# Taking kv from the value weights as column-group pairs, and moving five small transfers up the sync queue

## The chip, the cores and the metric

The kernel runs on one core of one Trainium2 chip. The metric is device time in microseconds (us), the median of several executions. The start of each matmul is recorded to a few nanoseconds.

## The reference, cut to what matters

The kernel computes `g * A(x) + (1 - g) * B(x)` for 2048 tokens of width 640. Path B is a two-layer mixer and MLP. Path A is linear attention with 32 heads of 20:

```python
qkv = (x @ wqkv) ...                      # 32 heads, Dh = 20
pq, pk = phi(q), phi(k)
kv  = einsum("bhsd,bhse->bhde", pk, v)    # one 20 x 20 matrix per head
num = einsum("bhqd,bhde->bhqe", pq, kv)
den = einsum("bhqd,bhd->bhq", pq, z) + 1e-6
A   = (num / den).reshape(B, S, D) @ wo
```

As v = x wv, kv per head is wv^T (x^T pk). The kernel builds `GT` = x^T pk once (640 x 640). It then takes only blocks of 60 x 60 (three heads) of wv^T GT, masks them to single heads (`Lt`), and multiplies them by wo, giving one matrix M. With M, path A is one matrix product per tile of normalised queries.

## The kernel before

The kernel has its own scheduler: work items are put in program order by their dependencies, and each engine is given its list in that order. TensorE runs the projections, GT, kv and M, then the MLP; ten "a" matmuls per token tile of 128 (two groups of five, for 512 and for 128 columns) apply M. The parts the change touches follow.

ScalarE copies the value weights into a regrouped form, so that one full 128-column weight load holds two blocks at rows 0 and 64:

```python
def wv_blocks(k):                 # 5 copies for each of 5 k: 25 ScalarE instructions
    ...
    activation(wv2[:, k, e:e + 2 * ns - 1:2, 64 * h:64 * h + 64], src, ACTF.Copy)
```

Then kv comes in two items, with another matmul group between them:

```python
KV0 = (0, 60, 240, 300, 480, 540)
def kvt_group(h):
    ...
    for q_, g in enumerate(range(4) if h == 0 else range(4, 6)):
        for k in range(KD):                       # KD = 5
            l = wv2[:, k, g, :]                   # 128 weight columns
            # 120 moving columns (two blocks), or 160, or 60
```

Of each 128 x 120 product only the two diagonal 60 x 60 blocks are used.

The last rows of M (the tail of each head pair) are computed into a small tile `Mt` and brought to rows 60 to 67 of `M_sb` by five transfers of 10 KB on the sync queue (SP). The same queue issues the DMA transposes of the normalised x (`xnT<-xn`) and of the queries (`pqnT<-pq_tok`, one per token tile):

```python
def m_tail():
    for j in range(KD):
        sch.dma("sp", M_sb[60:68, j, :], Mt[8 * j:8 * j + 8, :], "mt", group_total=KD)
...
IT.add("MT", ("mt",), 0.0, m_tail, deps=[(("m", 1), 1.5), (("qt", 5), 0.0)])   # behind the 6th query transpose
```

The first "a" group reads all of `M_sb`, so it waits for these five.

## Time and profile before

| what | value | from |
|---|---|---|
| time | 262.55 us, median of 3 | times |
| TensorE busy | 257.3 us of 261.4 (98%) | page, part 1 |
| kv matmuls | 1.05 + 0.48 = 1.53 us | starts in the trace |
| wait for M's last rows | 0.94 us | starts in the trace |
| ScalarE copies of the weights | 6.5 us | groups by form |

The page of the kernel before, part 1 (busy us, share, number of instructions) and part 4 (the chain that ended last):

```profile
PE 257.3 (98%) x1665; PEld 133.9 (51%) x1665; DVE 151.7 (58%) x289; ACT 112.1 (43%) x241; POOL 93.0 (36%) x152
...
PE 96%; DMA 2%; SPq 0%; DVE 0%; ACT 0%; issue 0%
```

TensorE is the bound; only what shortens its list, or a wait in it, can shorten the run. Busy time of a pipelined matmul overlaps its neighbours' (379 ns are recorded for one of 512 columns), so a better reading is the step from one matmul's start to the next: 216 ns for 512 columns, 56 ns for 128. Where a step is longer, TensorE waited, or it entered or left another form of its array (309 to 312 ns, see the prediction).

The timeline of TensorE around kv (start, us, engine, line, operation, shapes, count):

```profile
76.64 1.03 PE L601 MATMUL ps<-xnT,w 128*128 128x512 bf16 x4
77.50 1.21 PE L974 MATMUL ps<-GT,wv 128*128 128x120 bf16 x20
78.55 1.24 PE L601 MATMUL ps<-xnT,w 128*128 128x512 bf16 x5
79.63 0.65 PE L974 MATMUL ps<-GT,wv 128*128 128x160 bf16 x10
80.11 1.24 PE L601 MATMUL ps<-xnT,w 128*128 128x512 bf16 x5
```

Read the starts: kv takes 77.50 to 78.55 and 79.63 to 80.11.

The sync queue (timeline of SP) and TensorE around the first "a" group, then the waits that name the transfers:

```profile
123.41 3.08 SPq L281 DMA_TRANSPOSE xnT<-xn  x2
126.53 9.00 SPq L281 DMA_TRANSPOSE pqnT<-pq_tok  x6
135.66 4.13 SPq L285 DMA_DIRECT2D M_sb<-Mt  x5
139.88 2.54 SPq L281 DMA_TRANSPOSE xnT<-xn  x2
```

```profile
136.63 3.62 PE L601 MATMUL ps<-xnT,w 128*128 128x512 bf16 x16
141.03 1.53 PE L601 MATMUL ps<-M_sb,pqnT 128*128 128x512 bf16 x10 [0.78 <-DMA M_sb<-Mt]
```

```profile
PEld ps L601 <- DMA M_sb<-Mt: 1.3, 1, 1.3
...
PE ps L601 <- DMA M_sb<-Mt: 0.8, 1, 0.8
```

Six query transposes stand ahead of the transfers in the queue, though the first "a" group needs only one of them. The last matmul before the wait starts at 139.87, the next at 141.03: 1156 ns where 216 would do, so 0.94 us is lost. (The 0.78 of the view is counted from the modelled end of a matmul.)

### The profile page before, as it was taken

How to read it: one execution, taken by the hardware profiler on the slowest of the kernel's cores; microseconds unless marked ns; L12 is line 12 of the kernel's file. 1: busy time of each engine (PE TensorE's matmuls, PEld its weight loads, DVE VectorE, ACT ScalarE, POOL GpSimd, SP SyncE). 2: the span in 40 equal slices, each digit the busy share in tenths (PEclk: the TensorE clock that was granted, in tenths of full speed). 3: DMA queues.
4: the chain of work that ended last, by engine and by line, in shares of the span. 5: the costliest groups of instructions: out<-in, count | busy, mean ns of one | idle time of the engine just before them, and what ended most of it. 6: DMA issues, size and time to landing. Idle time of an engine off the chain costs nothing.

```text
span 261.4 us, 4276 instructions
## 1 busy us (share of the span) xinstructions
PE 257.3 (98%) x1665; PEld 133.9 (51%) x1665; DVE 151.7 (58%) x289; ACT 112.1 (43%) x241; POOL 93.0 (36%) x152
## 2 busy tenths in 40 slices
PE   8999999999999999999998999999999999999996
PEld 4655555554455555554444545654455644455453
DVE  1497787899903799998996406993023320133232
ACT  1386767759355766685853240005500035200000
POOL 4003996869864019667901401130011110021001
DMA  6865869582656991362572670123000020000211
GB/s 196 256 103 143 165 173 171 168 142 42 107 107 125 354 332 31 74 104 51 110 95 58 125 78 0 25 65 113 0 3 0 0 103 0 0 3 1 100 53 50
DMA packets 51348, 24.99 MB, mean 96 GB/s; under 512 B 42708, under 2 KB 49917, under 8 KB 51328
## 3 DMA queue, kind: packets, MB, share of 16 engines
q1 hardware_dynamic: 49952, 21.31, 35.4%
q0 software_dynamic: 1136, 3.28, 5.6%
q8 instruction: 13, 0.21, 0.3%
q10 hardware_dynamic: 240, 0.13, 0.2%
q14 instruction: 7, 0.06, 0.1%
HBM read 12.05 MB, written 2.62 MB: 56 GB/s over the span
## 4 chain that ended last, share of the span: by engine, by line
PE 96%; DMA 2%; SPq 0%; DVE 0%; ACT 0%; issue 0%
PE ps L601 60%; PE ps L1176 22%; PE ps L783 8%; PE ps L875 2%; DMA wq<-in_A_wqkv_dram 1%; PE ps L1088 1%; PE ps L1158 1%; DMA M_sb<-Mt 1%; PE ps L974 1%; PE ps L876 1%; SPq L285 0%; DVE x_tok L640 0%; PE ps L1006 0%; PE ps L612 0%; ACT h2T L657 0%; PE ps L1155 0%
## 5 line engine op out<-in xcount | busy, mean ns | idle before, releaser
L601 PE MATMUL ps<-xnT,w 128*128 128x512 bf16 x360 | 81.6, 379 | 0.0
L657 ACT ACTIVATE h2T<-ps 128x512 bf16<-128x512 f32 x52 | 30.5, 598 | 68.5 <-PE ps L601 68.5
L1176 PE MATMUL ps<-w,h2T 128*128 128x512 bf16 (+1 forms) x416 | 58.8, 299 | 0.0
L601 PEld LDWEIGHTS ps<-xnT,w 128*128 128x128 bf16 x360 | 34.2, 98 | 38.2 <-issue 0.9
L640 DVE SCALAR_TENSOR_TENSOR x_tok<-ps,stg,abx 128x512 bf16<-128x512 f32 (+1 forms) x32 | 17.3, 550 | 61.1 <-PE ps L1176 61.1
L623 POOL TENSOR_SCALAR abx<-x_tok,stg 128x640 f32<-128x640 bf16 x16 | 14.8, 928 | 97.5 <-DVE x_tok L640 94.2
L1176 PEld LDWEIGHTS ps<-w,h2T 128*128 128x128 bf16 x416 | 32.1, 98 | 24.9 <-issue 1.1
L623 POOL TENSOR_SCALAR xn<-x_tok,st 128x640 bf16<-128x640 bf16 x32 | 34.5, 1086 | 17.9 <-DMA xnT<-xn 17.2
L657 ACT ACTIVATE Er<-ps 128x640 bf16<-128x640 f32 x32 | 22.5, 705 | 18.5 <-PE ps L876 8.6
L601 PE MATMUL ps<-M_sb,pqnT 128*128 128x512 bf16 (+1 forms) x160 | 24.4, 299 | 0.8 <-DMA M_sb<-Mt 0.8
L656 ACT ACTIVATE junk<-x_tok 128x640 bf16<-128x640 bf16 x32 | 23.6, 737 | 3.1 <-DVE x_tok L638 2.6
L657 ACT ACTIVATE hsT<-ps 128x512 bf16<-128x512 f32 (+1 forms) x32 | 18.9, 593 | 13.4 <-PE ps L601 13.0
L601 PE MATMUL ps<-w,hsT 128*128 128x512 bf16 (+1 forms) x160 | 23.7, 299 | 0.0
L601 PE MATMUL ps<-wkg,xT 128*128 128x512 bf16 (+1 forms) x150 | 22.6, 299 | 0.0
L640 DVE SCALAR_TENSOR_TENSOR abx<-ps,stg,abx 128x640 f32<-128x640 f32 x16 | 14.1, 884 | 14.4 <-PE ps L601 7.4
L601 PEld LDWEIGHTS ps<-w,hsT 128*128 128x128 bf16 x160 | 13.3, 98 | 12.2
L601 PEld LDWEIGHTS ps<-M_sb,pqnT 128*128 128x128 bf16 x160 | 13.1, 98 | 11.9 <-DMA M_sb<-Mt 1.3
L601 PE MATMUL ps<-wq,xT 128*128 128x512 bf16 (+1 forms) x120 | 18.3, 299 | 0.0
L783 PE MATMUL ps<-pk_tok,x_tok 128*128 128x512 bf16 x80 | 17.8, 379 | 0.0
L623 DVE TENSOR_SCALAR Er<-Er 128x640 bf16<-128x640 bf16 x32 | 11.6, 362 | 9.4 <-ACT Er L657 9.2
L601 PEld LDWEIGHTS ps<-wkg,xT 128*128 128x128 bf16 x150 | 12.2, 97 | 9.0
L638 DVE SCALAR_TENSOR_TENSOR x_tok<-ps,x_tok 128x640 bf16<-128x640 f32 x16 | 13.1, 820 | 6.0 <-PE ps L601 5.1
(76 smaller groups left out, 241.1 us busy)
## 6 DMA issues: line engine op xcount, KB each, us to landing
w<-in_B_w_dram SPq DMA_DIRECT2D x1, 2160.0 KB, 8.2
w<-in_B_w_dram SPq DMA_DIRECT2D x1, 2080.0 KB, 15.1
x_tok<-in_A_x_dram SPq DMA_DIRECT2D x3, 640.0 KB, 5.7
out_dram<-x_tok SPq DMA_DIRECT2D x3, 640.0 KB, 3.1
w<-in_B_w_dram POOLq DMA_DIRECT2D x8, 160.0 KB, 4.4
wq<-in_A_wqkv_dram SPq DMA_DIRECT2D x5, 160.0 KB, 3.9
wkg<-in_A_wqkv_dram SPq DMA_DIRECT2D x5, 160.0 KB, 3.9
wv<-in_A_wqkv_dram POOLq DMA_DIRECT2D x1, 800.0 KB, 6.1
```

What stands on the lines that cost most here:

```text
L601: ins = e.matmul(out_ap, l, r, start=(i == 0), stop=(i == n - 1))
L623: return engf(lambda e: e.tensor_scalar(out_ap, in_ap, s1, s2, op0, op1), rd, [out_ap], cost=cost)
L638: return dve(lambda e: e.scalar_tensor_tensor(out_ap, in0, scalar, in1, op0, op1, accum_out=accum), rd, [out_ap, accum], cost=cost + 70.0)
L640: return dve(lambda e: e.scalar_tensor_tensor(out_ap, in0, scalar, in1, op0, op1), rd, [out_ap], cost=cost)
L656: return act(lambda e: e.activation(out_ap, in_ap, func, bias=bias, scale=scale, accum_out=accum), rd, wr, cost=cost)
L657: return act(lambda e: e.activation(out_ap, in_ap, func, bias=bias, scale=scale), rd, wr, cost=cost)
L783: ins = e.matmul(o, l, r, start=(t0 + q_ == 0), stop=(t0 + q_ == NT - 1))
L875: e.matmul(ps[:, b, 0:512], l, w[:, k, 0:512], start=(k == 0), stop=(k == KD - 1))
L876: return e.matmul(ps[:, b + 1, 0:n2], l, w[:, k, 512:512 + n2], start=(k == 0), stop=(k == KD - 1))
L974: ins = e.matmul(o, l, r_, start=st_, stop=sp_, skip_group_check=True)
L1088: ins = e.matmul(o, l, r, start=st, stop=sp)
L1176: ins = e.matmul(o, l, r, start=False, stop=(i == KFF - 1), skip_group_check=(n0 > 0))
```

## The change

Two things at once. First, kv: no regrouped copy. Each 60-row block takes 64 columns of the value weights where they lie; two blocks go to output rows 0 to 63 and 64 to 127, that is to two column groups of the array, which are meant to run at the same time. Second, the five transfers go behind the third query transpose instead of the sixth.

```diff
-    wv2 = ra.alias("wv2", [128, KD, 6, 128], BF16, ...)
...
-    def wv_blocks(k): ...            # and its 5 work items
...
-    KV0 = (0, 60, 240, 300, 480, 540)
+    KV0 = ((0, 120), (60, 180), (240, 360), (300, 420), (480, 600), (540, None))
-    def kvt_group(h):
+    def kvt_group():
...
+        for g, cs in enumerate(KV0):
             for k in range(KD):
-                l = wv2[:, k, g, :]
...
+                for h, c0 in enumerate(cs):
+                    if c0 is not None:
+                        n = min(B3, D - c0)
+                        mms.append((ps[64 * h:64 * h + 64, b, B3 * g:B3 * g + n], wvf[:, D * k + c0:D * k + c0 + 64],
+                                    GT[:, k, c0:c0 + n], g == 0 and k == 0, k == KD - 1))
...                                   # taking kv out of PSUM: 5 VectorE instructions instead of 7
-    IT.add("MT", ("mt",), 0.0, m_tail, deps=[(("m", 1), 1.5), (("qt", 5), 0.0)])
+    IT.add("MT", ("mt",), 0.0, m_tail, deps=[(("m", 1), 1.5), (("qt", 2), 0.0)])
...
-        IT.add("QT", ("qt", t), ..., deps=[...])
+        IT.add("QT", ("qt", t), ..., deps=[...] + ([(("mt",), 0.0)] if t == 3 else []))
```

More of the change, by code (lines that the diff above doesn't have):

```diff
@@ L495, in _build @@
     GT = ra.alias("GT", [128, KD, D], BF16, ra.last_addr, KD * S * 2)
-    wv2 = ra.alias("wv2", [128, KD, 6, 128], BF16, ra.last_addr + KD * D * 2, KD * (S - D) * 2)
     wkg = ra.alloc("wkg", [128, KD, NK], BF16)
@@ L934, in _build @@
         IT.add("GT", ("g", i), 1.08, lambda i=i: gt_step(i, NT - 5, NT), deps=[(("g0", NT - 1), 0.0)])
-    def wv_blocks(k):
-        def heads(lo, ns):
-            v = wvf[:, D * k + lo:D * k + lo + 240 * ns].rearrange("p (s c) -> p s c", s=ns)
-            return [v[:, :, 60 * e:60 * e + 64] for e in range(2)]
-        for h, ns in ((0, 3), (1, 2)):
-            for e, src in enumerate(heads(120 * h, ns)):
-                activation(wv2[:, k, e:e + 2 * ns - 1:2, 64 * h:64 * h + 64], src, ACTF.Copy)
-        src = wvf[:, D * k + 600:D * k + 664].unsqueeze(1).to_broadcast([128, 2, 64])
-        activation(wv2[:, k, 4:6, 64:128], src, ACTF.Copy)
-    for k in range(KD):
-        IT.add("WV", ("wv2", k), 0.0, lambda k=k: wv_blocks(k), deps=[(("k", NT - 1), 2.0), (("lwv",), 0.0), (("ga", 1), 0.0)])
-    kv_bank = {}
-    KV0 = (0, 60, 240, 300, 480, 540)
-    def kvt_group(h):
-        b = pair()
-        kv_bank[h] = b
-        bank_hold.update((b, b + 1))
+    kv_bank = {}
+    KV0 = ((0, 120), (60, 180), (240, 360), (300, 420), (480, 600), (540, None))
+    def kvt_group():
+        b = bank()
+        kv_bank[0] = b
+        bank_hold.add(b)
         mms = []
-        for q_, g in enumerate(range(4) if h == 0 else range(4, 6)):
-            c0 = KV0[g]
-            n1 = (B3, B3, B3, B3, 40, 0)[g]
+        for g, cs in enumerate(KV0):
             for k in range(KD):
-                l = wv2[:, k, g, :]
-                if n1 == 60:
-                    r_ = GT[:, k, c0:c0 + 240].rearrange("p (a c) -> p a c", a=2)[:, :, 0:B3]
-                    o = ps[:, b, 120 * q_:120 * q_ + 120].rearrange("p (a c) -> p a c", a=2)
-                    mms.append((o, l, r_, q_ == 0 and k == 0, k == KD - 1))
-                elif n1:
-                    mms.append((ps[:, b, 120 * q_:120 * q_ + 160], l, GT[:, k, c0:c0 + 160], q_ == 0 and k == 0, k == KD - 1))
-                else:
-                    mms.append((ps[:, b, 160:160 + B3], l, GT[:, k, c0:c0 + B3], False, k == KD - 1))
+                for h, c0 in enumerate(cs):
+                    if c0 is not None:
+                        n = min(B3, D - c0)
+                        mms.append((ps[64 * h:64 * h + 64, b, B3 * g:B3 * g + n], wvf[:, D * k + c0:D * k + c0 + 64], GT[:, k, c0:c0 + n],
+                                    g == 0 and k == 0, k == KD - 1))
         def fn(e):
@@ L975, in fn, with lt_evac, put @@
             return ins
-        pe(fn, [wv2[:, :, :, :], GT[:, :, :]], [ps[:, b, 0:480], ps[:, b + 1, 0:1]], cost=len(mms) * 60.0)
-    def lt_evac(h):
-        b = kv_bank[h]
-        def put(p0, q0, nq, dq, c0, step):
-            pr = slice(p0, p0 + B3)
-            o0 = 4 * (q0 % 2)
-            src = psf[pr, 512 * b + c0:512 * b + c0 + step * nq].rearrange("p (q c) -> p q c", q=nq)[:, :, 0:B3].rearrange("p q (a d) -> p q a d", d=DH)
-            dst = Lt[pr, q0:q0 + dq * (nq - 1) + 1:dq, o0:o0 + B3].rearrange("p q (a d) -> p q a d", d=DH)
-            tt(dve, dst, src, mask[pr, :, :].unsqueeze(1).to_broadcast([B3, nq, 3, DH]), ALU.mult)
-        if h == 0:
-            for e in range(2):
-                put(0, e, 2, 2, 120 * e, 240)
-                put(64, e, 2, 2, 120 * e + 60, 240)
-        else:
-            put(0, 4, 1, 2, 0, 160)
-            put(0, 5, 1, 2, 160, 160)
-            src = ps[64:104, b, 120:160].rearrange("p (h m i) -> p h m i", m=5, i=4)
-            tt(dve, Lt[64:104, 4, 0:40].rearrange("p (m h i) -> p h m i", m=5, i=4), src,
-               mask[64:104, 0:2, :].rearrange("p h (m i) -> p h m i", i=4), ALU.mult)
-        bank_hold.difference_update((b, b + 1))
+        pe(fn, [wvf[:, :], GT[:, :, :]], [ps[:, b, 0:360]], cost=1000.0)
+    def lt_evac():
+        b = kv_bank[0]
+        def put(p1, q0, nq):
+            o0 = 4 * (q0 % 2)
+            src = ps[0:p1, b, B3 * q0:B3 * (q0 + 2 * nq)].rearrange("p (q e c) -> p q e c", e=2, c=B3)[:, :, 0, :] if nq > 1 else \
+                ps[0:p1, b, B3 * q0:B3 * (q0 + 1)].unsqueeze(1)
+            dst = Lt[0:p1, q0:q0 + 2 * nq - 1:2, o0:o0 + B3].rearrange("p q (a d) -> p q a d", d=DH)
+            tt(dve, dst, src.rearrange("p q (a d) -> p q a d", d=DH), mask[0:p1, :, :].unsqueeze(1).to_broadcast([p1, nq, 3, DH]), ALU.mult)
+        put(128, 0, 2)
+        put(128, 1, 2)
+        put(B3, 4, 1)
+        put(B3, 5, 1)
+        src = ps[64:104, b, 240:280].rearrange("p (h m i) -> p h m i", m=5, i=4)
+        tt(dve, Lt[64:104, 4, 0:40].rearrange("p (m h i) -> p h m i", m=5, i=4), src,
+           mask[64:104, 0:2, :].rearrange("p h (m i) -> p h m i", i=4), ALU.mult)
+        bank_hold.discard(b)
     def m_step(jobs, tails):
@@ L1037, in zb_group @@
         copy(dve, zb[:, :], psf[:, 512 * b:512 * b + D])
-    for h in range(2):
-        IT.add("KVF", ("kvt", h), 0.0, lambda h=h: kvt_group(h), deps=[(("g", KD - 1), 1.0), (("wv2", KD - 1), 1.0)])
-        IT.add("KVF", ("lt", h), 0.0, lambda h=h: lt_evac(h), deps=[(("kvt", h), 0.0)])
+    IT.add("KVF", ("kvt", 1), 0.0, kvt_group, deps=[(("g", KD - 1), 1.0)])
+    IT.add("KVF", ("lt", 1), 0.0, lt_evac, deps=[(("kvt", 1), 0.0)])
     IT.add("KVF", ("m", 0), 0.0, m_last, deps=[(("lt", 1), 1.0), (("w1", 2, 2), 0.0)])
     IT.add("KVF", ("m", 1), 0.0, m_first, deps=[(("lt", 1), 1.0), (("w3", 0, 5), 0.0)])
-    IT.add("MT", ("mt",), 0.0, m_tail, deps=[(("m", 1), 1.5), (("qt", 5), 0.0)])
+    IT.add("MT", ("mt",), 0.0, m_tail, deps=[(("m", 1), 1.5), (("qt", 2), 0.0)])
     IT.add("ZB", ("zb",), 0.0, zb_group, deps=[(("z", NT - 1), 1.7), (("w2", 0), 0.0)])
@@ L1267, in _build @@
         IT.add("QN", ("qn", t), 0.0, lambda t=t: qn_scale(t), [(("qs", t), 0.0)])
-        IT.add("QT", ("qt", t), 0.0, lambda t=t: qt_tile(t), deps=[(("qn", t), 3.2), (("w2", NT - 1), 0.5), (("t2", 11 if t < 6 else NT - 1), 0.0)])
+        IT.add("QT", ("qt", t), 0.0, lambda t=t: qt_tile(t), deps=[(("qn", t), 3.2), (("w2", NT - 1), 0.5), (("t2", 11 if t < 6 else NT - 1), 0.0)] + ([(("mt",), 0.0)] if t == 3 else []))
     for t in range(NT):
```

## The prediction

> **What bounds the kernel.** TensorE. The page of the kernel before gives PE 257.3 us of a 261.4 us span (98%), and the chain of waits is PE for 96%. I compared the starts of successive matmuls in the trace with the usual steps (216 ns for 512 columns, 56 ns for 128). From 8 us to the last matmul they differ in few places: one wait of 0.94 us at 139.9 us, and about 0.1 us wherever the array enters or leaves its 64-row or 64-column form (309 to 312 ns instead of 216, then 10 to 20 ns on the next matmul). VectorE is 58% busy, ScalarE 43%: taking work from them is worth nothing here.
>
> **The wait.** The first attention tile needs rows 60 to 67 of M, brought by five small transfers. They sit behind the sixth query transpose in the sync queue (timeline of SP): transposes 126.5 to 135.5 us, transfers 135.7 to 139.8, last landing 140.97. TensorE could have gone on at 140.09. M itself is out of PSUM by 129.4.
>
> **What the change does.**
>
> 1. Transfers behind the third query transpose. That is issued by about 130.5, so the transfers are issued from 130.5 to 134.7 and land by about 136.5, 3.5 us ahead of need. Removes 0.94 us of the critical path. Three normalised-x transposes and query transposes 4 to 6 change places with them; the last x transpose should be out by 144 (145 before) and is needed at 151 or later. The TensorE order is otherwise the same. I expect no new wait.
>
> 2. kv. Before: 30 full-width matmuls in two groups, 1.05 + 0.48 = 1.53 us (52.5 ns for 120 columns, 69 for 160, 27.5 for 60). After: 55 matmuls of 60 columns on 64-column weights, 25 pairs and 5 singles, so 30 steps. If weight loads hide, a step costs the 27.5 ns of a 60-column matmul: 0.83 us. Entering and leaving costs 0.22 us, by the two-column-group matmuls at 150.6 us: 1.05 us in all, a gain of 0.5. The Trainium skill, "TensorEngine Tiling (Array Packing)", Restrictions, says that column tiling disables Fast Weight Load, and "TensorE: Matmul & The Clock Gate", LDWEIGHTS, gives columns/1.2 ns: 53 ns for 64 columns (an estimate from that page). With that exposed, 30 steps take 1.6 + 0.22 = 1.8 us, a loss of 0.3. This trace has 64-column loads only under 128- or 512-column matmuls; recorded loads are 103 to 110 ns against 98 for full width, a difference of some 10 ns, not of 27, which favours hiding. I take 35 to 40 ns a step as middle: 1.3 us, a gain of 0.25.
>
> 3. 25 ScalarE copies (6.5 us) go: off the path, worth nothing. VectorE evacuates kv in five operations instead of seven: nothing.
>
> **Sum.** 262.55 - 0.94 - 0.25 = 261.35 us. I predict 261.3, with 80% between 260.8 and 262.0. Faster by over 2%: 0.01; within 2%: 0.98; slower by over 2%: 0.01.
>
> **What would show each step.**
> - PE waits: the line naming the M_sb<-Mt transfers gone, last transfer landing near 136.5; step at the first attention tile 216 ns.
> - Starts of the kv matmuls: pair-to-pair 27 to 40 ns, the group 0.85 to 1.2 us plus two bubbles of 0.09 us; above 50 ns means weight loads are exposed.
> - ScalarE busy down by 6.5 us, span not following.
> - No new PE wait at 140 to 160 us.
>
> **What would make it wrong.** Weight loads of the two column groups serialising (over 100 ns a pair: the kv gain becomes a loss above 1.5 us); instruction supply failing at four instructions per 27 ns; the reordered sync queue delaying x transposes 13 to 16 or query transposes 5 and 6; other PSUM banks chosen after kv, bringing a wait for an evacuation.

## The result

| | median | range | runs |
|---|---|---|---|
| before | 262.39 us | 261.57 to 262.55 | 6 |
| changed | 260.86 us | 260.68 to 260.98 | 6 |

The ratio is 0.9945 (95% interval 0.9931 to 0.9958), and the result is correct. Ratios here are the mean time of one kernel's fast runs over that of the other's fast runs of the same rounds, so they are not quite the ratio of the medians. Executions over 1.5% slower than the fastest of the same kernel are left out of the means.

The page of the changed kernel, parts 1 and 4:

```profile
PE 255.7 (99%) x1690; PEld 132.2 (51%) x1690; DVE 151.7 (58%) x287; ACT 106.8 (41%) x216; POOL 92.8 (36%) x152
...
PE 97%; DMA 1%; DVE 0%; SPq 0%; issue 0%
```

There are 25 more matmuls (1690) in less TensorE time, and 25 fewer ScalarE instructions. Around kv (TensorE's timeline):

```profile
76.33 0.81 PE L600 MATMUL ps<-xnT,w 128*128 128x512 bf16 x3
77.07 1.13 PE L954 MATMUL ps<-GT,wv 128*64 128x60 bf16 x55
78.14 2.12 PE L600 MATMUL ps<-xnT,w 128*128 128x512 bf16 x9
```

The sync queue and TensorE at the first "a" group:

```profile
125.52 4.55 SPq L281 DMA_TRANSPOSE pqnT<-pq_tok  x3
130.18 3.69 SPq L285 DMA_DIRECT2D M_sb<-Mt  x5
134.33 1.23 SPq L281 DMA_TRANSPOSE pqnT<-pq_tok  x1
135.67 3.85 SPq L281 DMA_TRANSPOSE xnT<-xn  x3
```

```profile
135.75 3.62 PE L600 MATMUL ps<-xnT,w 128*128 128x512 bf16 x16
139.20 1.52 PE L600 MATMUL ps<-M_sb,pqnT 128*128 128x512 bf16 x10
```

The bracket with the wait is gone: the step before the first "a" matmul is 216 ns, and no wait naming the transfers is left in the view. The kv matmuls lie in one stretch, with steps of 31.7 ns from pair to pair and 2 to 4 ns inside a pair.

Where did the time go between the two profiles? The last matmul starts at 259.16 us before and at 257.32 after, 1.84 us earlier. Four terms read from starts add up to it:

| term | us | how it is read |
|---|---|---|
| before kv | 0.52 | the matmul ahead of kv starts at 77.28 and at 76.76 |
| kv | 0.37 | from that matmul to the one after kv: 2.829 less the 1.079 of the group between, against 1.376 |
| first full-size matmul after kv | -0.01 | 226 ns instead of 216 |
| the wait | 0.95 | 1156 and 227 ns, against 216 and 216 |

The first term is not the change's: TensorE's instructions up to there are the same, and it arises before 12.4 us. The profile before has steps of 107 ns instead of 56 up to 7.1 us, the other one only up to 3.8 us, which makes 0.95 us; a step of 486 ns at 11.3 us in the latter takes 0.43 back. In eleven other profiles below, that matmul starts anywhere between 76.3 and 77.2 us, and the two profiles of the kernel before have it at 77.28 and 76.70. The start of the program varies by half a microsecond and more. So this pair of profiles shows 1.3 us of gain from the change and half a microsecond of luck.

### The profile page after: what moved, and what is told of

Read it like the earlier page. It is cut to its first block, busy times and chain, and to the rows that moved or that the text cites. A ratio compares the mean times of both kernels' runs of the same rounds, so it can differ in the third digit from the quotient of the medians.

```text
span 259.6 us, 4300 instructions
## 1 busy us (share of the span) xinstructions
PE 255.7 (99%) x1690; PEld 132.2 (51%) x1690; DVE 151.7 (58%) x287; ACT 106.8 (41%) x216; POOL 92.8 (36%) x152
## 4 chain that ended last, share of the span: by engine, by line
PE 97%; DMA 1%; DVE 0%; SPq 0%; issue 0%
PE ps L600 61%; PE ps L1152 22%; PE ps L782 8%; PE ps L874 2%; DMA wq<-in_A_wqkv_dram 1%; PE ps L1064 1%; PE ps L1134 1%; PE ps L875 1%; DVE x_tok L639 0%; PE ps L954 0%; PE ps L983 0%; SPq L285 0%; PE ps L611 0%; PE ps L1131 0%; PE ps L847 0%
```

## The experiments

The theory after the result: kv gives 0.36 us (0.37 less the 0.01 after it), the transfers 0.94 us, both pieces of TensorE time. The rivals: a part of the gain is from elsewhere (ScalarE's copies, the start); the wait only moves on; kv is set by instruction issue and not by pairing. In some of these profiles 31 matmul records are missing, none of them in the kv stretch. "kv stretch" below is from the first to the last start of kv matmuls.

| run | median of the fast runs, us | ratio to before (95%) | kv stretch, us | step before the first "a" matmul, ns |
|---|---|---|---|---|
| changed, again | 261.02 | 0.9964 (0.9951 to 0.9976) | 0.939 | 215 |
| transfers only | 261.20 | 0.9970 (0.9958 to 0.9982) | as before | 216 |
| kv only | 261.39 | 0.9977 (0.9964 to 0.9990) | 0.940 | 714 |
| copies kept | 260.82 | 0.9943 (0.9913 to 0.9973) | 0.940 | 216 |
| groups one after the other in a block | 260.75 | 0.9965 (0.9943 to 0.9988) | 0.940 | 216 |
| transfers behind the fifth | 260.81 | 0.9942 (0.9911 to 0.9974) | 0.939 | 216 |
| one column group (wrong result) | 261.72 | 0.9983 (0.9952 to 1.0015) | 1.731 | 216 |
| sixty columns | 260.92 | 0.9939 (0.9912 to 0.9966) | 0.892 | 216 |
| groups wholly apart | 261.53 | 0.9964 (0.9930 to 0.9999) | 1.631 (slow profile) | - |

Rows 1, 2, 3 and 5 share their runs of the kernel before (median 262.03), as do rows 4, 6 and 7 (262.13), and rows 8 and 9 (262.28). The kernel before scattered more in the later rounds (261.03 to 264.00), which widens the intervals there; the medians of the runs in the same table group compare better than the ratios across groups.

### The change again, and its two parts

> The change once more, beside its parts on the same chip. Theory (the two gains are separate pieces of TensorE time and add): 1.3 us below the kernel before, 0.94 from the wait for M's last rows and 0.37 from kv (1.53 us of matmuls before; 1.17 us after, with entering and leaving the two-column-group form). A ratio of 0.995. Rival (part of the 1.5 us between the medians is something that start-to-start times in the middle of the trace do not show, as the start of the program): clearly more than 1.3 us, with the rest before 14 us of the trace.

Measured: 0.9964, about 0.94 us by the means; the expected 0.995 lies just outside the interval. The first rounds gave 0.9945, the rounds together 0.9 to 1.4 us, on both sides of the 1.3 us of the trace's steps. The traces agree better than the times once the start is left out: from the matmul ahead of kv to the first "a" matmul it is 63.74 and 63.67 us in the two looks at the kernel before, and 62.44 us in both of the changed one. The rival, a gain clearly above 1.3 us, fell: what exceeded it in the first pair of profiles was the start, as shown above.

The transfers alone (kernel before, two lines):

```diff
-    ... m_tail, deps=[(("m", 1), 1.5), (("qt", 5), 0.0)])
+    ... m_tail, deps=[(("m", 1), 1.5), (("qt", 2), 0.0)])
-    ... qt_tile(t), deps=[...])
+    ... qt_tile(t), deps=[...] + ([(("mt",), 0.0)] if t == 3 else []))
```

> The kernel before with only the five transfers moved behind the third query transpose. Theory: 0.94 us below the kernel before (ratio 0.9964); the long start-to-start step before the first attention tile (1156 ns) becomes 216; last transfer landing near 136. Rival (the wait only moves on, to a query or normalised-x transpose that now comes later in the sync queue): less than 0.5 us, with a new step over 216 ns between 140 and 160 us.

Measured: 0.9970, 0.8 us; the expected 0.9964 lies within the interval. Only the sync queue's order differs from the kernel before; all other engines' lists are the same. Its timeline at the first "a" group shows no wait:

```profile
133.65 5.99 PE L601 MATMUL ps<-xnT,w 128*128 128x512 bf16 x26
139.47 1.52 PE L601 MATMUL ps<-M_sb,pqnT 128*128 128x512 bf16 x10
```

The wait did not move on: no step from 140 to 160 us is longer than in the kernel before, apart from pairs of steps that hide a missing record.

kv alone (the changed kernel, with those two lines put back):

> The changed kernel with the five transfers put back behind the sixth query transpose. Theory A (VectorE's query work, and so the transfers, run behind TensorE's own progress and come earlier with it): 0.37 us below the kernel before (ratio 0.9986), the wait for the transfers still 0.9 us. Theory B (the transfers land at a time that kv does not move, so the wait eats what kv saves): no gain, the wait 1.3 us.

Measured: 0.9977, 0.6 us. The interval still holds theory A's 0.9986, but the trace shows more than either theory had: the kv stretch gave its 0.36 us, and the wait also shrank, from 0.94 us to 0.50 (a step of 714 ns). To see whether this was chance, both kernels were looked at once more:

> The kernel before, one more look at the wait for M's last rows, which was 0.94 us in its first profile. Theory (the wait is a race between the sync queue and TensorE, and changes from run to run with single transposes whose issue takes 1.9 to 2.4 us instead of 1.3): between 0.3 and 1.2 us, and not the same as 0.94; the kv stretch the same to a few ns.

> The run with kv alone, one more look: in its first profile the wait was 0.50 us and one transpose's issue was stretched by 0.6 us. Theory (a race): again between 0.3 and 1.2 us. Rival (kv alone shortens the wait, as ScalarE's copies no longer hold up what feeds the transfers): 0.50 again, to 0.05 us.

The first "a" group in kv alone, then in its second look, then in the second look at the kernel before:

```profile
139.90 1.53 PE L600 MATMUL ps<-M_sb,pqnT 128*128 128x512 bf16 x10 [0.34 <-DMA M_sb<-Mt]
```

```profile
139.97 1.53 PE L600 MATMUL ps<-M_sb,pqnT 128*128 128x512 bf16 x10 [0.37 <-DMA M_sb<-Mt]
```

```profile
140.37 1.53 PE L601 MATMUL ps<-M_sb,pqnT 128*128 128x512 bf16 x10 [0.71 <-DMA M_sb<-Mt]
```

In steps the waits are 0.50 and 0.54 us for kv alone, and 0.94 and 0.87 for the kernel before. All four lie in the range that my theory of a race allowed, but the two looks at each kernel agree to 0.04 and 0.07 us, so it was hardly chance from run to run: kv alone shortens the wait by about 0.4 us. The two gains are not independent. In the traces, from the matmul ahead of kv to the first "a" matmul, the transfers alone give 0.94 us and kv alone 0.81, together more than the 1.30 of the whole.

What shortens it can be read in the sync queue. A query transpose takes 1.28 us to issue; in each trace one issue is stretched. In the kernel before it is the fourth query transpose, and in the changed kernel and in kv alone it is the second. The stretched issue of before, of after and of kv alone:

```profile
130.51 2.38 SPq L281 DMA_TRANSPOSE pqnT<-pq_tok  x1
```

```profile
126.84 1.91 SPq L281 DMA_TRANSPOSE pqnT<-pq_tok  x1
```

```profile
127.21 1.89 SPq L281 DMA_TRANSPOSE pqnT<-pq_tok  x1
```

The stretch is 1.1 us in the kernel before and 0.6 here (0.8 in the second look at kv alone). In the first look at kv alone that is all of the 0.4, in the second about two thirds; there the query transposes also began some 0.15 us earlier against TensorE. In thirteen traces the stretched issue begins within 0.4 us of one fetch on DMA queue q8: the fetch starts at 130.54 us before, 126.52 after and 126.84 for kv alone, and in the run with the transfers alone at 129.89, where the stretched issue is the first of the five transfers (1.42 us instead of 0.78). The DMA view of such a stretch of the kernel before (130.3 to 131.0 us):

```profile
q8 instruction: 1, 0.02, 11.4%
```

Queue q8 makes 13 fetches, 0.21 MB in all; divided by the 3330 matmuls and weight loads of the kernel before that is 64 bytes each, so it is most likely TensorE's own instruction stream, fetched 16 KB (128 pairs of load and matmul) at a time. The kept traces bear that out: counted from the matmul ahead of kv, this fetch comes after 53.3 us in the kernel before and 53.2 with the transfers alone, which has the same TensorE list, and after 49.8 us in the changed kernel and also with ScalarE's 25 copies put back. So it follows TensorE's list and not ScalarE's. The 25 more matmuls of the new kv make the fetch come 3 us earlier relative to M, where it stretches another transpose, and less. In the kernel before the stretched issue starts together with the fetch (130.51 and 130.54 us); in the changed kernel and in kv alone it starts 0.3 to 0.4 us into it; all three end 2.2 to 2.4 us after the fetch began. A later start within the fetch would thus explain the smaller stretch. This is read from coincidence in the traces; no run moved the fetch by itself, so the cause is not shown.

### How far up the queue is far enough

The changed kernel with the transfers behind the fifth query transpose:

```diff
-    ... m_tail, deps=[(("m", 1), 1.5), (("qt", 2), 0.0)])
+    ... m_tail, deps=[(("m", 1), 1.5), (("qt", 4), 0.0)])
-    ... if t == 3 ...
+    ... if t == 5 ...
```

> The changed kernel with the five transfers behind the fifth query transpose instead of the third (behind the sixth in the kernel before). In the two traces with them behind the sixth the first attention tile waited 0.94 and 0.50 us, and one transpose's issue takes 1.3 us. Theory (the wait is only a matter of the place in the queue): one place earlier is 1.35 us earlier, which covers both; no wait, the time of the changed kernel within 0.2 us, with 0.4 to 0.9 us of slack left, so an occasional slower run. Rival (the wait depends on when VectorE finishes the query tiles, and any place after the fourth waits): a wait of 0.3 us or more.

Measured: 260.81 us, no wait, a step of 216 ns. The transfers in its trace (durations of the issues in ns; first and last start in us):

```profile
L285 SPq DMA_DIRECT2D M_sb<-Mt x5: 624/642/776, 132.7 to 136.2; - x5
```

The last is issued 2.6 us before the first "a" matmul (138.78). In the kernel before the last issue came at 139.16 and landed 1.8 us later, so the slack here is about 0.7 us (an estimate from that landing). The wait was a matter of place in the queue; in the changed kernel one place would have done, three leave room.

### ScalarE's copies

The changed kernel, with the 25 copies made as before and read by nobody:

```diff
+    wv2 = ra.alias("wv2", ...)
+    def wv_blocks(k): ...            # as in the kernel before, with its 5 work items
```

> The changed kernel with the 25 copies of the value weights on ScalarE still made, and read by nobody. Theory (ScalarE has room, the copies are off the path): the time of the changed kernel within 0.15 us, ScalarE busy 6.5 us more. Rival (the copies push ScalarE's GT and gelu work back, and taking them away was part of the gain): 0.2 us or more above the changed kernel, with new long steps between matmuls from 70 to 80 us.

Measured: 260.82 us, against 260.81 of the run beside it. Part 1 of its page:

```profile
PE 254.4 (98%) x1659; PEld 132.8 (51%) x1690; DVE 151.5 (58%) x287; ACT 112.1 (43%) x241; POOL 92.5 (36%) x152
```

ScalarE is 5.3 us busier than in the changed kernel, and the time is the same: the copies were off the path. The rival fell.

### What the pairs give

The changed kernel with each block's five matmuls of one column group before the five of the other:

```diff
-            for k in range(KD):
-                for h, c0 in enumerate(cs):
+            for h, c0 in enumerate(cs):
+                for k in range(KD):
```

> The changed kernel with the same 55 small matmuls in another order: for each block first the five of one column group, then the five of the other, so that no two neighbours share a step. Theory (two column groups do run at once, a pair costs the step of one): 55 steps of 31.5 instead of 30, 0.79 us above the changed kernel. Rival (the small matmuls are bound by the issue of instructions, about 16 ns for a load and a matmul, and pairing gains nothing): within 0.1 us of the changed kernel.

Measured: no loss at all (260.75 us; two of the six runs were slower, 261.53 and 262.57, and have no trace), with the same stretch of 0.940 us. The loss that the theory forecast did not come, and taken alone this is what the rival said. But the starts decide against the rival. They still come in pairs, 4 to 6 ns apart, and the moving sizes in order of start do not follow the program. The program has 45 matmuls of 60 columns (both groups), then five of 40 (second group), then five of 60 (first group). The end of the trace's list, by recorded start in ns, is:

```
77416 40 cols    77420 60    77447 40    77452 60    77479 40    77483 60
77511 40         77515 60    77542 40    77547 60    77578 60    77610 60    77642 60
```

After the first 40 stand eight of 60 instead of five: three that the program has ahead of it were overtaken. After the last 40 stand four: one that the program has behind it came before it. TensorE started matmuls of one column group ahead of earlier ones of the other. So this edit had not separated the pairs, and a stricter one was needed. First, everything in one column group (the sums mix, so the result is wrong):

```diff
-  mms.append((ps[64 * h:64 * h + 64, b, ...
+  mms.append((ps[0:64, b, ...
```

> The changed kernel with all 55 small matmuls, in their order, in the first column group (the result is wrong on purpose: both blocks of a pair add into the same sums). The run with the blocks' order changed did not slow down, and its records show 40-column matmuls of the second group between 60-column ones of the first that come later in the program, so there the two groups still ran side by side. Theory (a pair costs one step only because its two matmuls are in different column groups): 55 steps of about 31.6 ns instead of 30, the kv stretch 1.74 us instead of 0.95, 0.79 us above the changed kernel (ratio to the kernel before near 1). Rival (the step is set by issue, some 16 ns for a load and a matmul, and the groups do not matter): the stretch stays 0.95 us and the time that of the changed kernel.

The kv group in its timeline:

```profile
77.00 1.93 PE L954 MATMUL ps<-GT,wv 128*64 128x60 bf16 x55
```

The stretch is 1.731 us, 0.79 more than 0.940, in even steps of 31.7 ns, and the time is 0.9 us above the two good kernels in the same rounds (260.81 and 260.82). Pairing does give the 0.79 us; without it the new kv would be slower than the old one (1.53 us).

Second, the right result again, in the order: all 30 matmuls of the first group, then all 25 of the second.

```diff
+        for h in range(2):
             for g, cs in enumerate(KV0):
                 for k in range(KD):
-                    for h, c0 in enumerate(cs):
+                    c0 = cs[h]
```

> The changed kernel with the 55 small matmuls in the order: all 30 of the first column group, then all 25 of the second. When each block's five came group by group, they still ran in pairs. Theory A (TensorE's queue reaches far enough ahead to take the second group's work out of order over 60 instructions): the second group starts at once or soon, the stretch stays about 0.95 to 1.1 us. Theory B (it reaches only some ten or twenty instructions ahead): the second group starts when the first is nearly through, 45 steps or more of 31.7 ns, 1.4 us or more.

```profile
79.19 1.82 PE L955 MATMUL ps<-GT,wv 128*64 128x60 bf16 x55
```

Theory B holds, with a reach even shorter than it said. This profile fell in the slow state (270.18 us, with 512-column steps of 224 ns instead of 216), but its kv steps are still 31.7 ns, and the three fast runs (261.39, 261.53 and 261.71 us) are some 0.7 us above the changed kernel's level, as 1.631 against 0.940 says. In the starts 26 matmuls run alone before the first pair: the second group's first matmul starts with the 27th of the first, when three of it are left. In the run with the blocks' order changed, it started with the second of five, again with three left. In both orders TensorE passed over three matmuls and their loads and no more.

### What sets the step of 31.7 ns

The changed kernel with other sizes per block pair (wrong result):

```diff
+    SHAPES = ((64, 60), (64, 32), (48, 60), (48, 32), (60, 40), (64, 60))   # weight columns, moving columns
-                        n = min(B3, D - c0)
+                        wc, n = SHAPES[g]
```

> The changed kernel with other sizes of weights and moving columns in each block pair (wrong result on purpose): pairs of weight columns x moving columns 64x60, 64x32, 48x60, 48x32, 60x40, and five singles of 64x60. Theory (a 64-column weight load takes longer than 60 columns stream, so the load sets the step of 31.7 ns: columns/2.4 + 5 ns): steps of 31.7, 31.7, 27.5 (there the stream's own time), 25, 30. Rival (the stream of 60 columns with a cost of its own in this form sets it): 31.7, 20, 31.7, 20, 23.

Measured, from the starts (mean of the steps inside each block pair; the very first step, 54 ns, is left out):

| weight x moving columns | 64x60 | 64x32 | 48x60 | 48x32 | 60x40 |
|---|---|---|---|---|---|
| expected by the load | 31.7 | 31.7 | 27.5 | 25 | 30 |
| expected by the stream | 31.7 | 20 | 31.7 | 20 | 23 |
| measured, ns | 31.7 | 31.8 | 26.8 | 25.8 | 30.0 |

The number of weight columns sets the step: about halving the moving columns changes nothing, and taking a quarter of the weight columns does. That it is the load of these columns that takes the time is the plain reading; no run shows a load's own duration in the stream. That points to a version with 60-column loads, as rows 60 to 63 of a block are never used:

```diff
-  ps[64 * h:64 * h + 64, b, ...], wvf[:, D * k + c0:D * k + c0 + 64]
+  ps[64 * h:64 * h + n, b, ...],  wvf[:, D * k + c0:D * k + c0 + n]
-        put(128, 0, 2); put(128, 1, 2)            # 128 rows in one VectorE instruction
+        for e in range(2): put(0, e, 2); put(64, e, 2)    # 60 rows each
```

> The changed kernel with weight loads of 60 (and 40) columns instead of 64, as rows 60 to 63 of each block are never used; VectorE takes kv out in seven pieces of 60 rows instead of five. The result must stay right. In the run with other sizes, pairs of 60 weight columns stepped by 30.0 ns and pairs of 64 by 31.7. Theory (the weight load sets the step): steps of 30.0 to the last, the kv stretch shorter by 0.05 us than in the changed kernel; the time the same within the noise (0.05 us is 0.02%). Rival (the 30.0 came from the 40 moving columns of that probe): steps of 31.7.

```profile
77.50 1.08 PE L954 MATMUL ps<-GT,wv 128*60 128x60 bf16 x55
```

The result is correct, the steps are 30.0 ns, and the stretch is 0.892 us, 0.05 less than 0.940. The five matmuls with 40-column loads, all in the second group, stepped by 25.0 ns while the first group beside them kept its 30.0. So columns/2.4 + 5 ns, which would give 21.7, does not reach down to 40 columns. The time (260.92 us, ratio 0.9939) cannot be told from the changed kernel's, as expected for 0.02%. It is the shortest TensorE list of all, by a margin that only the trace can show.

## Why the prediction was right or wrong

The predicted time was 261.3 us, 80% between 260.8 and 262.0; measured 260.86 in the first rounds and 261.02 in the second. The call "within 2%" was right, and so was the mechanism: two pieces of TensorE time, read from steps between starts.

- **The wait.** Predicted 0.94 us, gone. It is gone, and the profile that was predicted from had 0.94. Other runs of the kernel before have less (0.87 in the second look). The transfers were issued from 130.2 (predicted 130.5) to 133.9 rather than 134.7, as one gap of 1.17 us between the starts of two issues became 0.79. The fear that the reordered queue would delay x transposes did not come true.
- **kv.** The middle of 0.25 us was too cautious; it measured 0.36. The mis-sized term is the step: I took 35 to 40 ns, between the hidden load (27.5) and the 53 ns worked out from the skill page, and it is 31.7. Neither branch held: the weight columns do set the step, but at three fifths of the page's figure. The value between them was a compromise and not derived, so its nearness is in part luck. The cost of entering and leaving the two-column-group form, put at 0.22 us, measured 0.09 + 0.02 + 0.095 + 0.01 = 0.22: 309 ns instead of 216 going in, a first step of 54 instead of 32, 127 instead of 32 coming out, and 226 instead of 216.
- **"Nothing" for ScalarE and VectorE.** Shown for ScalarE by the run with the copies kept, and for VectorE by the run with sixty columns, which has seven evacuations again (260.92 us). ScalarE's busy time fell by 5.3 us, not by 6.5: single copies overlap in the records.
- **The sum.** It treated the two parts as independent. They are not quite: kv alone also shortens the wait, by some 0.4 us, in part probably through the time of an instruction fetch (not shown). For the whole change this does not count, as the wait is zero anyway; but for one part alone it does.
- **Noise.** The text did not reckon with the start of the program, which moves by half a microsecond between runs. It made the first difference (1.5 us by the medians) look larger than the 1.3 us that the change's own steps account for. The second rounds showed 0.9 to 1.0.

## What to carry to other kernels

Look at what a late, tiny transfer stands behind in its issuing queue: five 10 KB transfers cost 0.9 us only because of transposes ahead of them that nobody needed yet, and moving up by one place would have been enough in the changed kernel. Splitting a wasteful full-width matmul into column-group pairs paid here when the pairs were neighbours in program order, or at most about three matmuls apart. Judge it with the weight load, not the stream, as the cost of a step (31.7 ns here, where the stream alone would take 27.5). When an effect is below the scatter of the times, read it from start-to-start steps in the trace, and check one edit's records before concluding from its time: the edit that should have taken the pairs apart had not done so.

## What the Trainium skill lacked or had wrong

- "TensorE: Matmul & The Clock Gate", LDWEIGHTS: it gives columns/1.2 ns, which is 53 ns for 64 columns. Pairs of 64-column loads stepped by 31.7 ns, 60 by 30.0 and 48 by 25.8, and two column groups loaded in the same time as one (single steps 31.7). Columns/2.4 + 5 ns fits these three to a nanosecond, but not the 25.0 ns measured with 40 columns.
- The same page, Part 3, "What overlaps and what doesn't": it calls matmuls "strict FIFO, no reordering". With the groups one after the other in a block, 40-column matmuls of the second column group started before three 60-column ones of the first that stand earlier in the program, by up to 67 ns.
- The same page, on queue depth: it names a reorder window of 64 that pulls weight loads ahead. Here matmuls of the other column group were taken out of order only past three matmuls and their loads; with 30 in front, 26 ran alone first (stretch 1.631 us instead of 0.940).
- The same page, Back-to-back issue gap: it states about 81 ns per matmul of 128 columns and 131 for 512 in a stream with weight loads. This kernel's streams, each matmul with its load, step by 56 and 216 ns.
- "TensorEngine Tiling (Array Packing)", Key Properties and Restrictions: that a change of mode drains the array and that column tiling disables the fast weight load agrees, but no size is given. A visit to the form of two column groups cost 0.22 us, and the step rose from 27.5 ns (60 moving columns on 128-column loads, full width) to 31.7 on 64-column loads.
- "Runtime: NRT & Kernel Launch", Instruction fetch mechanics: it has the fetch, in blocks of 16 KiB over a DMA queue of its own, and calls its cost "mostly hidden". It doesn't say what the fetch does to the kernel's own transfers. Here one fetch of 16 KB coincided with an issue of a transpose of 1.9 to 2.4 us instead of 1.28 (argued from coincidence in the traces, not tested).
